# Half-empty 64-row passes of the third weight, run in pairs in the two row halves of the array

## The chip, the cores and the metric

The kernel runs on one core of a Trainium2 chip. The metric is the device time of one execution, in microseconds (us). Three runs of the kernel before took 371.08, 371.08 and 371.23 us; their median is 371.08.

The engines go by the profile's names: PE is the matrix engine (PEld its weight loads, which are instructions of their own), DVE the vector engine, ACT the scalar engine, POOL the general one, SP the engine that issues most DMAs. SBUF is the memory of 128 partitions in which tiles lie; PSUM is the smaller one that PE writes to, with 8 banks of 128 x 512 fp32.

## The reference

An input of 2048 tokens by D = 448 channels goes through two branches that are mixed by a gate. Branch `a` is a long convolution (a state-space filter). Branch `b` is what the change touches:

```python
h = _gelu(_layernorm(x) @ w1)                 # D x D
hs = shifted(h) @ w2                          # four channel groups moved by +1, -1, +2, -2 tokens
x1 = x + hs
h2 = _gelu(_layernorm(x1) @ w3) @ w4          # D x F, then F x D, F = 1792
b = x1 + h2
out = g * a + (1 - g) * b                     # g = sigmoid(sum(x * gate_w))
```

D = 448 is three tiles of 128 rows and one of 64. That last tile of 64 rows is the change's subject.

## The kernel before

**Precision.** Every matmul of a weight is made of three products in the type fp32r. An operand is split into a high part (rounded to fp32r) and a low part (what is left): `w3h`, `w3l` for the weight, `XH`, `XL` for the input. high x high, low weight x high input, and high weight x low input are added in one PSUM bank.

**The 64 rows.** The contraction over 448 channels takes four tiles, k = 0 to 3. In tile k = 3 only 64 rows are real. The kernel fills the other half: the weights are stored twice (rows 0 to 63 and again 64 to 127), and `XH[:, 3]` holds the input's high part in rows 0 to 63 and its low part in rows 64 to 127. So one pass of `w3h[:, 3]` over `XH[:, 3]` gives high x high and high x low together, which is why `XL` has three tiles only. The pass of `w3l[:, 3]` over the same tile gives low x high in its first half, and low x low in its second, a product that is left out for all other tiles.

**Units.** The work is cut into 72 units (line 455): 16 of kind `a` (w1 and w2, four channel groups in each of four blocks of 512 tokens), then 56 of kind `d` (w3 and w4: 14 tiles of F in each of four blocks). For a unit of kind `d`, `first(n)` makes 11 passes of 512 columns into a bank `p1` (L478), ACT applies the gelu into `uf` (L539) and copies it into `uh` (L549), DVE forms the low part `ul` (`act_tail`, L569), and `second(n)` makes 12 passes of 448 columns into the four banks `acc0` to `acc3` (L603), which stay open over the 14 units of a block. At a block's end `residual` adds them to the tokens `xs` on DVE.

**Order.** All is written out by hand, in program order for each engine. A loop over n (line 1217) issues, in this order: DVE's low part of the next unit (`act_tail(n + 1)`, for n from 14 on; before that it comes after the `after` list), tasks of the lists `before` and `after`, `first(n + 2)`, gelu and copy of unit n + 2, the list `between`, some steps of the filter's recurrence (`ssm_some`, DVE scans with ACT scalings), the list `late`, and `second(n)`. Each engine works through its own instructions in that order; semaphores between them follow from the tiles. The lists hold the splitting of w3 and w4 (`part_hi` on ACT, `part_lo` on DVE), the layernorm of x1 for the next block (`norm_...`), and the filter's preparation. ACT splits into the high part, DVE subtracts to get the low one.

**Buffers that matter here.** Three PSUM banks go round under the tag `p1`, one is called `misc`, four are `acc`. In SBUF `uh` and `ul` have three buffers each.

The first unit of kind `d` is number 16; `first(16)` is issued in the loop's step 14, behind `second(13)` and ahead of `second(14)`. Its layernormed input comes back from a turn through DRAM into `NT_`, and `norm_hi` (L448, ACT) and `norm_lo` (L409, L410, DVE) fill `XH` and `XL`.

Of the kernel before, what the change touches and what calls it, by code (L numbers as in the profile page):

```python
# [8 lines left out]
F32 = mybir.dt.float32  # L9
F32R = mybir.dt.float32r  # L10
I32 = mybir.dt.int32
AF = mybir.ActivationFunctionType
# [8 lines left out]
TB = 512  # L21
NB = L // TB
# [6 lines left out]
NF = F // 128  # L29
# [6 lines left out]
LAG = 2  # L36
# [143 lines left out]
def mixer_and_small_steps(ctx, tc, xs, gg, okm, x, xT, xb, x0, w1, w2, w3, w4, gate, par, logdt, dskip, ident, out):  # L180
    nc = tc.nc

    big = ctx.enter_context(tc.tile_pool(name="big", bufs=1))
    wk = ctx.enter_context(tc.tile_pool(name="wk", bufs=2))
    ps = ctx.enter_context(tc.tile_pool(name="ps", bufs=2, space=PSUM))
# [13 lines left out]
    w3l = big.tile([128, 4, F], F32R, name="w3l")  # L199
# [173 lines left out]
    XH, XL = {}, {}  # L373
# [71 lines left out]
    def norm_hi(b, i):  # L445
        if i == 0:
            hl_tiles(("d", b))
        nc.scalar.activation(XH["d", b][:, :, i * 128:(i + 1) * 128], NT_[b, i], AF.Copy)  # L448

    def weigh(b, i):  # L450
        j = NT * b + i
        nc.scalar.activation(xs[:, j, :], xs[:, j, :], AF.Copy, scale=gs[:, j:j + 1])


    units = [("a", b, g) for b in range(NB) for g in (0, 2, 1, 3)] + \
            [("d", b, f) for b in range(NB) for f in range(NF)]
    w4 = dict(src=w4)
    W4 = {}
    P1, UF, UH, UL, ACC = {}, {}, {}, {}, {}

    def first(n, bank="p1", seq=None, stop=True):

        kind, b, i = units[n]
        xh, xl = XH[kind, b], XL[kind, b]
        if kind == "a":
            wh, wl = (w1d, None) if i == 2 else (w1h[:, TI[i]], w1l[:, TI[i]])
            o = HALO - SHIFT[i]
        else:
            wh, wl = (w[:, :, i * 128:(i + 1) * 128] for w in (w3h, w3l))
            o = 0  # L470
        fresh = n not in P1
        if fresh:
            P1[n] = ps.tile([128, TB], F32, name="p1", tag=bank, bufs=3 if bank == "p1" else 1)
        p = P1[n]
        every = [(w, x_, k, 0, TB) for x_, ks in ((0, (0, 1, 2)), (0, (3,)), (1, (0, 1, 2))) for w in range(2 - x_)
                 for k in ks if not w or wl is not None]
        for q, (w, x_, k, t0, t1) in enumerate(seq or every):
            nc.tensor.matmul(p[:, t0:t1], (wl if w else wh)[:, k, :], (xl if x_ else xh)[:, k, o + t0:o + t1],  # L478
                             start=(q == 0 and fresh), stop=stop if q + 1 == len(seq or every) else False)
# [15 lines left out]
    def mul_ops(n):  # L495

        kind, b, i = units[n]
        p, o = P1[n], b * TB + HALO - SHIFT[i]
        MUL.add(n)
        if i == 2:  # L500
            if n not in UF:
                act_add(n, False)
                yield
                act_add(n, True)
                yield
            nc.vector.tensor_mul(UF[n][:GD], UF[n][:GD], rb[:GD, o:o + TB])
        else:
            UF[n] = wk.tile([128, TB], F32, name="uf")
            nc.vector.tensor_mul(UF[n], p, rb[:, o:o + TB])
        yield  # L510
# [4 lines left out]
    def head_ops(n):  # L515
        kind, b, i = units[n]
        if kind == "a" and n not in MUL:
            yield from mul_ops(n)
        UH[n] = wk.tile([128, TB], F32R, name="uh", bufs=3)
        if kind == "a" and i == 2:  # L520
            nc.scalar.activation(UF[n][:GD], UF[n][:GD], AF.Gelu_apprx_tanh)
            yield
        elif kind == "a":
            UL[n] = wk.tile([128, TB], F32R, name="ul", bufs=3)
            o, sk = SHIFT[2] - SHIFT[i], skew[:, TI[i], :]
            uf, UF[n] = UF[n], big.tile([128, TB], F32, name="ug", tag="w4bl")
            nc.scalar.activation(UF[n], uf, AF.Gelu_apprx_tanh)
            yield
            if n:
                nc.scalar.activation(UF[n][:GX, :o], sk[:, SKEW - o:], AF.Gelu_apprx_tanh)  # L530
                yield
            nc.scalar.activation(UF[n][:GX, o:], uf[:GX, :TB - o], AF.Gelu_apprx_tanh)
            if b + 1 < NB:
                EDGE[n] = sk, uf[:GX, TB - SKEW:]
            yield
        else:
            UL[n] = wk.tile([128, TB], F32R, name="ul", bufs=3)
            UF[n] = wk.tile([128, TB], F32, name="uf")
            nc.scalar.activation(UF[n], P1[n], AF.Gelu_apprx_tanh)  # L539
            yield  # L540
# [14 lines left out]
    def act_head(n, later=False):  # L555
        drain(head_ops(n))
        if not later:
            drain(copy_ops(n))

    def act_copy(n):  # L560
        drain(copy_ops(n))

    def act_tail(n):
        kind, b, i = units[n]
        uf = UF.pop(n)
        if kind == "a" and i == 2:
            nc.vector.tensor_sub(UH[n][GD:], uf[:GD], f32(UH[n])[:GD])
        else:
            nc.vector.tensor_sub(UL[n], uf, f32(UH[n]))  # L569
# [161 lines left out]
        nc.vector.tensor_reduce(rk[:, 4:5], rk[:, 0:4], axis=AX.X, op=OP.min)  # L731

    def ssm_mask():
        p = ps.tile([128, 1], F32, name="misc", bufs=1)
        nc.tensor.matmul(p, one.to_broadcast([128, 128]), rk[:, 4:5], start=True, stop=True)
        nc.vector.tensor_copy(rk[:, 5:6], p)
        nc.vector.tensor_scalar(okm, rk[:, 5:6].to_broadcast([128, 16]), 127.5, None, op0=OP.is_ge)
        nc.vector.copy_predicated(nu.rearrange("p a b -> p (a b)"), okm, nuf.rearrange("p a b -> p (a b)"))
# [83 lines left out]
    def at(n, fn, *a, when=after):  # L822
        when.setdefault(n, []).append((fn, a))

    def run(when, n):
        for fn, a in when.pop(n, []):
            fn(*a)
# [184 lines left out]
    def first_head_ops():  # L1012

        UH[0] = wk.tile([128, TB], F32R, name="uh", bufs=3)
        UL[0] = wk.tile([128, TB], F32R, name="ul", bufs=3)
        uf, ug = UF[0], big.tile([128, TB], F32, name="ug", tag="w4bl")
        UG.append(ug)
        o = SHIFT[2] - SHIFT[0]
        for a_, c in HALVES:
            nc.scalar.activation(ug[:, a_:c], uf[:, a_:c], AF.Gelu_apprx_tanh)  # L1020
            yield
            q = max(a_, o)
            nc.scalar.activation(ug[:GX, q:c], uf[:GX, q - o:c - o], AF.Gelu_apprx_tanh)  # L1023
            yield
            nc.scalar.activation(UH[0][:, a_:c], ug[:, a_:c], AF.Copy)
            yield
        P1.pop(0)
        nc.scalar.activation(skew[:, TI[0], :], uf[:GX, TB - SKEW:], AF.Copy)
        yield
# [155 lines left out]
    for b in range(NB):  # L1185
        s0 = (7, 18, 31, 46)[b]
        for i in range(NT):
            n = s0 + (3, 4, 5, 3)[b] * (i // 2)
            if b:
                at(n, norm_d, b, i, when=late if b == 3 else after)  # L1190
                at(n + 1, norm_turn, b, i)
                at(n + 2, norm_fetch, b, i)
            q, when = n + (4 if b in (1, 2) else 3), late if b == 3 else before
            if b:
                at(q, norm_hi, b, i, when=when)
                at(q, norm_lo, b, i, when=when)
            at(max(s0 + i + 8, 28 + i // 2), weigh, b, i)
    at(16, ssm_par, 0)
    at(25, ssm_par, 1, when=late)
    at(17, ssm_exp, 0)  # L1200
# [14 lines left out]
    with tc.manual_schedule():  # L1215
        begin()
        for n in range(4, len(units)):
            if n >= 4 * NB - 2 and n + 1 < len(units):
                act_tail(n + 1)
            run(before, n)  # L1220
            spent = sum(cost.get(fn, 0.0) for when in (after, late) for fn, _ in when.get(n, []))
            run(after, n)
            if n < 4 * NB - 2 and n not in (7, 11):
                act_tail(n + 1)
            if n + LAG < len(units):
                first(n + LAG)
                if units[n + LAG][::2] == ("a", 2):
                    act_add(n + LAG, False)
            if n in (7, 11):
                second(n)  # L1230
                act_tail(n + 1)
            if n + LAG in UF:
                act_add(n + LAG, True)
            if n < OWN:
                run(between, n)
            if n + LAG < len(units) and n not in (6, 10):
                act_head(n + LAG, True)
            run(between, n)
            if n + LAG < len(units) and n not in (6, 10):
                act_copy(n + LAG)  # L1240
            if n >= OWN:
                ssm_some(n, 3.75 - (2.2 if units[n][2] == NF - 1 else 0.0) - spent)
            run(late, n)
            if n < len(units) - 2 and n not in (7, 11):
                second(n)
        last_two()
# [55 lines left out]
```

## Time and profile before

| | |
|---|---|
| timed runs | 371.08, 371.08, 371.23 us |
| span of the profiled execution, from the first to the last instruction | 368.9 us |
| median of the timed runs less that span: what lies around it | 2.2 us |
| DMA queues, all together | 46.14 MB, 125 GB/s mean |
| ACT's idle time ahead of the gelu of L539, ended by PE | 113.2 us in 49 waits |
| DVE's idle time ahead of the `ul` of L569, ended by ACT's `uh` | 23.0 us in 17 waits |
| smallest and largest time of a pass of 448 columns over `ul` and `w4h` | 357 and 373 ns |

The profile gives the span of one execution and no total of its own; a sum is therefore made on the span, and the 2.2 us are added to compare it with timed runs. Times in a row of the timeline are the start from the span's beginning and how long the record lasts; "x3" merges three instructions in a row, and the time is then of all of them. The record of a matmul is longer than the distance to the next, since matmuls are pipelined. A bracket at a row's end names the idle time of that engine just before, and what ended it. Groups show busy time in all, the mean of one in ns, and idle time before them.

### The profile page before, as it was taken

What the parts mean: (1) busy time and instruction counts of PE and PEld (TensorE: products, weight loads), DVE (VectorE), ACT (ScalarE), POOL (GpSimd) and SP (SyncE); (2) the same over time, 40 slices, a digit from 0 to 9 for tenths busy, and PEclk for the clock granted to TensorE, in tenths of its full rate; (3) what the DMA queues carried; (4) which work ended last, traced back from release to release, by engine and by line L of the source; (5) the groups of instructions that cost most, each with busy time, mean ns of one, the idle gap of its engine ahead of it and who ended that gap; (6) DMA issues with size and microseconds to landing.
All of it is one profiled execution on the core that took longest, in us unless ns stands there. A gap on an engine that the chain in (4) does not pass through costs nothing.

```text
span 368.9 us, 5308 instructions
## 1 busy us (share of the span) xinstructions
PE 363.4 (99%) x1734; PEld 314.3 (85%) x1734; DVE 308.1 (84%) x571; ACT 215.9 (59%) x383; POOL 63.3 (17%) x176
## 2 busy tenths in 40 slices
PE   8999999999999999999999999999999999999995
PEld 4988888888888888888888888888888888888885
DVE  4999979797999997378799899998789999998533
ACT  5987668777684637944274774554756645455220
POOL 1000432000300000110013433224243234000000
PEclk9999999999999999999999999999999999999999
DMA  7994116626948064001833514457385611361213
GB/s 258 393 398 157 38 65 124 134 88 251 390 134 203 0 116 156 0 0 52 178 107 77 89 28 94 114 165 131 83 131 121 179 16 28 79 179 30 64 50 105
DMA packets 88479, 46.14 MB, mean 125 GB/s; under 512 B 67200, under 2 KB 82944, under 8 KB 87808
## 3 DMA queue, kind: packets, MB, share of 16 engines
q1 hardware_dynamic: 88016, 45.27, 45.6%
q10 hardware_dynamic: 432, 0.49, 0.4%
q8 instruction: 15, 0.25, 0.3%
q14 instruction: 16, 0.13, 0.1%
HBM read 34.74 MB, written 11.01 MB: 124 GB/s over the span
## 4 chain that ended last, share of the span: by engine, by line
PE 93%; DMA 4%; ACT 1%; DVE 0%; ACTq 0%; SPq 0%; issue 0%
PE p L478 46%; PE acc L603 45%; DMA raw<-xb_in 2%; DMA xs<-x_in 2%; PE acc L638 1%; ACT xh L394 1%; PE p L638 0%; PE misc L363 0%; DVE xh L401 0%; ACT uf L996 0%; ACTq L268 0%; DVE uf L1007 0%; SPq L279 0%; ACT ug L1020 0%; ACT ug L1023 0%
## 5 line engine op out<-in xcount | busy, mean ns | idle before, releaser
L539 ACT ACTIVATE uf<-p 128x512 f32<-128x512 f32 x56 | 33.4, 597 | 113.3 <-PE p L478 113.2
L478 PE MATMUL p<-xh,w3l 128*128 128x512 f32 x224 | 70.1, 394 | 0.0
L478 PE MATMUL p<-xh,w3h 128*128 128x512 f32 x224 | 70.1, 394 | 0.0
L758 DVE TENSOR_TENSOR_SCAN z<-z,carry 128x512 f32<-128x512 f32 x48 | 61.5, 1282 | 4.2 <-POOL z L752 0.5
L603 PE MATMUL acc<-w4l,uh 128*128 128x448 f32 x216 | 56.3, 367 | 0.0
L603 PE MATMUL acc<-w4h,uh 128*128 128x448 f32 x216 | 56.0, 365 | 0.0
L603 PE MATMUL acc<-w4h,ul 128*128 128x448 f32 x216 | 55.8, 364 | 0.0
L569 DVE TENSOR_TENSOR ul<-uf,uh 128x512 fp32r<-128x512 f32 x56 | 38.1, 681 | 20.1 <-ACT uh L549 20.0
L478 PEld LDWEIGHTS p<-xh,w3l 128*128 128x128 f32 x224 | 42.1, 188 | 9.8
L478 PE MATMUL p<-xl,w3h 128*128 128x512 f32 x168 | 47.7, 392 | 0.0
L478 PEld LDWEIGHTS p<-xh,w3h 128*128 128x128 f32 x224 | 42.1, 188 | 6.6
L603 PEld LDWEIGHTS acc<-w4h,uh 128*128 128x128 f32 x216 | 40.5, 188 | 6.0
L603 PEld LDWEIGHTS acc<-w4h,ul 128*128 128x128 f32 x216 | 40.6, 188 | 3.5
L603 PEld LDWEIGHTS acc<-w4l,uh 128*128 128x128 f32 x216 | 40.6, 188 | 3.4
L753 ACT ACTIVATE z<-zs,nu 128x512 f32<-128x512 f32 x64 | 42.3, 710 | 0.6 <-DMA zs<-xT_in 0.6
L478 PEld LDWEIGHTS p<-xl,w3h 128*128 128x128 f32 x168 | 31.5, 188 | 7.2
L549 ACT ACTIVATE uh<-uf 128x512 fp32r<-128x512 f32 x56 | 35.4, 633 | 1.8
L752 POOL COPY z<-carry 128x1 f32<-128x1 f32 x48 | 32.1, 679 | 16.0 <-DVE zs L764 15.9
L760 POOL COPY carry<-z 128x1 f32<-128x1 f32 x48 | 13.1, 273 | 105.7 <-DVE z L758 105.0
L344 POOL TENSOR_TENSOR t<-r 128x4 f32<-128x4 f32 (+1 forms) x5 | 3.1, 627 | 117.4 <-DVE r L343 117.4
L603 PE MATMUL acc<-w2l,uh 128*128 128x448 f32 x64 | 19.9, 368 | 0.0
L758 DVE TENSOR_TENSOR_SCAN z<-z,carry,zero 128x512 f32<-128x512 f32 x16 | 19.9, 1247 | 0.0
(207 smaller groups left out, 541.8 us busy)
## 6 DMA issues: line engine op xcount, KB each, us to landing
zs<-xT_in SPq DMA_DIRECT2D x4, 1024.0 KB, 8.3
yd<-yt SPq DMA_DIRECT2D x56, 64.0 KB, 2.0
ysb<-yd SPq DMA_DIRECT2D x16, 224.0 KB, 2.7
raw<-xb_in SPq DMA_DIRECT2D x3, 1032.0 KB, 12.6
raw<-w_in SPq DMA_DIRECT2D x3, 1024.0 KB, 5.6
xd<-xt SPq DMA_DIRECT2D x16, 192.0 KB, 2.1
xr<-xd SPq DMA_DIRECT2D x16, 192.0 KB, 3.1
raw<-w_in SPq DMA_DIRECT2D x3, 896.0 KB, 4.6
```

The source lines that it names most:

```text
L344: eng.tensor_mul(t, y, y)
L394: nc.scalar.activation(XH["a", b][:, k, :], raw[b][:, k, :], AF.Copy)
L478: nc.tensor.matmul(p[:, t0:t1], (wl if w else wh)[:, k, :], (xl if x_ else xh)[:, k, o + t0:o + t1], start=(q == 0 and fresh), stop=stop i ...
L539: nc.scalar.activation(UF[n], P1[n], AF.Gelu_apprx_tanh)
L549: nc.scalar.activation(UH[n], UF[n], AF.Copy)
L569: nc.vector.tensor_sub(UL[n], uf, f32(UH[n]))
L603: nc.tensor.matmul(ACC[j], (UL if p == 2 else UH)[n][:, t], wl if p == 1 else wh, start=first_, stop=last_)
L638: nc.tensor.matmul(acc, (UL if p == 2 else UH)[m][:, t], (wl if p == 1 else wh)[:, c], start=q == last and m == n and p == 0, stop=m > n a ...
L752: nc.gpsimd.tensor_copy(z4[:, m, 0:1], carry[:, k, m:m + 1])
L753: nc.scalar.activation(z4[:, m, 1:], ZS[b][:, k, :], AF.Copy, scale=nu[:, k, m:m + 1])
L758: nc.vector.tensor_tensor_scan(z, z, up, carry[:, k, m:m + 1], OP.add, OP.add)
L760: nc.gpsimd.tensor_copy(carry[:, k, m:m + 1], z[:, TB - 1:])
```

## The change

The pass of `w3l[:, 3]` is no longer made in `first` for units of kind `d`. Instead, a new function `tails` makes it for up to four units at once (14 units of a block: 4, 4, 4 and 2), before `first` of the first of them. It uses only the 64 rows that carry low weight x high input; low x low of that tile is no longer computed. Even units of a group use rows 0 to 63 of `w3l` and of `XH`. Odd ones use rows 64 to 127 of `w3l` (the second copy of the weights) and a new tile `xt3`, in whose rows 64 to 127 `spread_tail` puts a copy of the high part (ACT, once per block). Each pass of `tails` opens the bank of its unit, and `first` then adds to it; three banks of a group are `p1`, the fourth is `misc`. For this `ssm_mask` moves from `misc` to `p1`, and `ul` gives up one of three buffers for the room of `xt3`.

```diff
+    def spread_tail(b):
+        XT[b] = big.tile([128, TB], F32R, name="xt3", tag="xt3")
+        nc.scalar.activation(XT[b][64:], XH["d", b][:64, 3, :TB], AF.Copy)
...
+    def tails(n):
+
+        kind, b, i = units[n]
+        for m in range(4 if i + 4 <= NF else 2):
+            last = m == 3
+            p = P1[n + m] = ps.tile([128, TB], F32, name="p1", tag="misc" if last else "p1", bufs=1 if last else 3)
+            t = slice((i + m) * 128, (i + m + 1) * 128)
+            if m % 2:
+                nc.tensor.matmul(p, w3l[64:, 3, t], XT[b][64:], start=True, stop=False)
+            else:
+                nc.tensor.matmul(p, w3l[:64, 3, t], XH[kind, b][:64, 3, :TB], start=True, stop=False)
...
-                 for k in ks if not w or wl is not None]
+                 for k in ks if not w or wl is not None and not (k == 3 and kind == "d")]
...
-            UL[n] = wk.tile([128, TB], F32R, name="ul", bufs=3)
+            UL[n] = wk.tile([128, TB], F32R, name="ul", bufs=2)
...
-        p = ps.tile([128, 1], F32, name="misc", bufs=1)
+        p = ps.tile([128, 1], F32, name="p1", tag="p1", bufs=3)
...
+    for b in range(NB):
+        at((13, 27, 41, 55)[b], spread_tail, b)
...
+                if units[n + LAG][0] == "d" and units[n + LAG][2] % 4 == 0:
+                    tails(n + LAG)
                 first(n + LAG)
```

Lines behind the insertions move by 6 to 22: `first` is L496 instead of L478, `second` L621 instead of L603, the gelu L557, the copy L567, the low part L587, the splits L958 and L961. `tails` is L475 (odd units) and L477 (even units), `spread_tail` L454.

On PE, in step 14, the end of `second(13)` and `first(16)` stood like this before (`p_1043` is unit 16's bank, `acc` are the banks of `second`; a bracket names the engines or DMAs that a row waits for):

```order
L603 MATMUL acc_995<-w2l,uh 128x448
L603 MATMUL acc_999<-w2l,uh 128x448
L478 MATMUL p_1043<-xh,w3h 128x512 [waits PE_49]
L478 MATMUL p_1043<-xh,w3h 128x512
L478 MATMUL p_1043<-xh,w3h 128x512 [waits Activation_49]
L478 MATMUL p_1043<-xh,w3l 128x512 x2
L478 MATMUL p_1043<-xh,w3l 128x512 [waits DVE_49]
L478 MATMUL p_1043<-xh,w3h 128x512
L478 MATMUL p_1043<-xh,w3l 128x512
L478 MATMUL p_1043<-xl,w3h 128x512 x3
```

and stand like this in the change (`p_1045`, `p_1047`, `p_1049` and `p_1051` are the banks of units 16 to 19, `xt_1009` is the copy):

```order
L621 MATMUL acc_995<-w2l,uh 128x448
L621 MATMUL acc_999<-w2l,uh 128x448
L477 MATMUL p_1045<-xh,w3l 128x512 [waits DVE_49,PE_49]
L475 MATMUL p_1047<-xt_1009,w3l 128x512 [waits Activation_49]
L477 MATMUL p_1049<-xh,w3l 128x512 [waits DVE_49]
L475 MATMUL p_1051<-xt_1009,w3l 128x512
L496 MATMUL p_1045<-xh,w3h 128x512 x3
L496 MATMUL p_1045<-xh,w3l 128x512 x3
L496 MATMUL p_1045<-xh,w3h 128x512
L496 MATMUL p_1045<-xl,w3h 128x512 x3
```

Four passes stand ahead of `first(16)` now, the second of them with a wait for ACT and the third with one for DVE; `first` has ten passes instead of eleven.

On ACT the copy that this second pass reads stands behind the splits of step 13, and ahead of the gelu of unit 15 (`ug`, with its short pieces for shifted channels), in the change:

```order
L567 ACTIVATE uh<-ug 128x512 [waits PE_49,Activation_49]
L958 ACTIVATE w4h_701<-raw 128x896
L958 ACTIVATE w3h<-raw 128x2x512 [waits DMAHW6_49]
L454 ACTIVATE xt_1009<-xh 64x512
L545 ACTIVATE ug<-uf 128x512 [waits DVE_49,Activation_49]
L548 ACTIVATE ug<-skew 16x4 [waits Activation_49]
L550 ACTIVATE ug<-uf 16x508
```

The row at L454 is new there; the others keep their order.

On DVE, around the low part of unit 16 (the second `ul` row here), the rows before are these:

```order
L569 TENSOR_TENSOR ul<-ug,uh 128x512 [waits Activation_49]
L943 TENSOR_TENSOR w4l_702<-raw,w4h_701 128x896
L943 TENSOR_TENSOR w3l<-raw,w3h 128x2x512 [waits DMAHW6_49]
L569 TENSOR_TENSOR ul<-uf,uh 128x512 [waits Activation_49]
L943 TENSOR_TENSOR w3l<-raw,w3h 128x2x512
```

and those of the change:

```order
L587 TENSOR_TENSOR ul<-ug,uh 128x512 [waits Activation_49]
L961 TENSOR_TENSOR w4l_702<-raw,w4h_701 128x896
L961 TENSOR_TENSOR w3l<-raw,w3h 128x2x512 [waits DMAHW6_49]
L587 TENSOR_TENSOR ul<-uf,uh 128x512 [waits DVE_49,PE_49,Activation_49]
L961 TENSOR_TENSOR w3l<-raw,w3h 128x2x512
```

The order is the same; unit 16's low part now also waits for PE, since its buffer is that of unit 14, which `second(14)` reads.

More of the change, by code (lines that the diff above doesn't have):

```diff
@@ L448, in norm_hi @@
         nc.scalar.activation(XH["d", b][:, :, i * 128:(i + 1) * 128], NT_[b, i], AF.Copy)
+    XT = {}
+    def spread_tail(b):
+        XT[b] = big.tile([128, TB], F32R, name="xt3", tag="xt3")
+        nc.scalar.activation(XT[b][64:], XH["d", b][:64, 3, :TB], AF.Copy)
     def weigh(b, i):
@@ L536, in head_ops @@
         else:
-            UL[n] = wk.tile([128, TB], F32R, name="ul", bufs=3)
+            UL[n] = wk.tile([128, TB], F32R, name="ul", bufs=2)
             UF[n] = wk.tile([128, TB], F32, name="uf")
@@ L1014, in first_head_ops @@
         UH[0] = wk.tile([128, TB], F32R, name="uh", bufs=3)
-        UL[0] = wk.tile([128, TB], F32R, name="ul", bufs=3)
+        UL[0] = wk.tile([128, TB], F32R, name="ul", bufs=2)
         uf, ug = UF[0], big.tile([128, TB], F32, name="ug", tag="w4bl")
```

## Prediction

> **What bounds the kernel now.** I read the page's busy shares first, then its chain of waits, then stretches of the timeline.
>
> ```profile
> PE 363.4 (99%) x1734; PEld 314.3 (85%) x1734; DVE 308.1 (84%) x571; ACT 215.9 (59%) x383; POOL 63.3 (17%) x176
> PEclk9999999999999999999999999999999999999999
> PE 93%; DMA 4%; ACT 1%; DVE 0%; ACTq 0%; SPq 0%; issue 0%
> 80.55:85.54 4.99, 4.99 (x25) 4.32 (x24) 2.55 (x4) 4.89 (x9) 0.00 (x0) 1.00 0.66 211
> 225.30:295.13 69.83, 69.83 (x324) 60.53 (x322) 62.62 (x77) 40.31 (x67) 21.68 (x45) 1.00 0.61 134
> ```
>
> TensorE is busy in 99% of the span at full clock, and the chain that ended last runs over it for 93%. The last two rows are stretches of the window view (length, then busy time of PE, PEld, DVE, ACT and POOL): one unit, and fourteen units of the steady part. PE is busy in all of both. So a unit costs 69.83 / 14 = 4.99 us, nothing hides a PE delay, and every PE saving counts until another engine is late; DVE is next, at 62.62 / 14 = 4.47 us a unit.
>
> What fills a unit is seen at the place where the second kind of unit begins (timeline of PE: start, time, instruction, count).
>
> ```profile
> 80.14 0.57 PE L603 MATMUL acc<-w2l,uh 128*128 128x448 f32 x2
> 80.55 0.85 PE L478 MATMUL p<-xh,w3h 128*128 128x512 f32 x3
> ...
> 81.94 0.40 PE L478 MATMUL p<-xh,w3h 128*128 128x512 f32 x1
> 82.17 0.39 PE L478 MATMUL p<-xh,w3l 128*128 128x512 f32 x1
> 82.41 0.86 PE L478 MATMUL p<-xl,w3h 128*128 128x512 f32 x3
> 83.10 0.36 PE L603 MATMUL acc<-w2h,uh 128*128 128x448 f32 x1
> ```
>
> From 80.55 to 83.10 stand eleven passes of 512 columns: 2.55 / 11 = 0.232 us each, though the record of one is 0.39 long, so matmuls overlap. The two of 448 columns before them are 0.57 - 0.36 = 0.21 apart; I use 0.20, since twelve fill 4.99 - 2.55. The pass at 82.17 is the one that the change takes out.
>
> **The change part by part.** *What it removes.* In each of the 56 units of the second kind that pass goes: 56 x 0.232 = 13.0 us. *What it adds on PE* is 28 pairs of 64-row passes, in 12 groups of four and 4 of two. If two halves really run together, a pair costs one pass, and 28 x 0.232 = 6.5 us is the most that can be won.
>
> *The switch of the array's shape.* Every group makes PE go from 128-row passes to 64-row ones and back. The trace holds one such change of tile, by columns: four products for the first tokens at L845, 2 columns wide, recorded as eight passes. PE first, then the weight loads.
>
> ```profile
> 11.96 0.28 PE L478 MATMUL p<-xh,w1h 128*128 128x256 f32 x1
> 12.17 0.39 PE L845 MATMUL pe<-w1r,xz 128*2 128x32 f32 x8
> 12.49 0.39 PE L478 MATMUL p<-xl,w1h 128*128 128x256 f32 x1
> ...
> 12.17 0.26 PEld L845 LDWEIGHTS pe<-w1r,xz 128*2 128x2 f32 x8
> 12.49 0.30 PEld L478 LDWEIGHTS p<-xl,w1h 128*128 128x128 f32 x2
> ...
> 31.87 0.60 PE L363 MATMUL misc<-idt,r 128*128 128x128 f32 x4
> ...
> 200.22 0.62 PEld L478 LDWEIGHTS p<-xh,w3h 128*128 128x128 f32 x3
> 200.41 0.86 PE L478 MATMUL p<-xh,w3h 128*128 128x512 f32 x3
> ```
>
> Elsewhere weights load beside the matmul before theirs: of the last two rows the load starts 0.19 before its pass. At the change of shape they don't: the first load comes at 12.17, 0.21 after the last full matmul started and 0.07 before its record ends (11.96 + 0.28); and the way back is alike, 12.49 against 12.17 + 0.39 = 12.56. The shape of the array changes only when the matmuls in it are nearly out, and the next weights load in the open. A load of 128 columns takes 0.11: four small matmuls stand 0.11 apart ((0.60 - 0.27) / 3). So, by the records of 0.36 and 0.39, the first 64-row pass starts 0.36 - 0.07 + 0.11 = 0.40 after the last 448-column pass, not 0.20; and the next full pass 0.39 - 0.07 + 0.11 = 0.43 after the last 64-row pass, not 0.23. **Each switch costs 0.20**. No row shows a switch of row halves: from below its price is 0, from above I keep 0.20, and I take the upper end as the nearest row. Inside a group the second half can start only when its own weights are in, 0.11 later, and that stagger stays to the end of the group (bounds 0 and 0.23, the latter meaning that halves don't overlap at all).
>
> A group of four thus costs 2 x 0.20 + 0.11 and saves 2 x 0.23: +0.05. A group of two saves 0.23: +0.28. Eleven of the first kind (the twelfth is next) and four of the second: 0.5 + 1.1 = **+1.6 us**. The Trainium skill, TensorEngine Tiling (Array Packing), Tiling Modes (Key Properties), says that changing the tiling mode, unlike changing the tile, drains the TensorE; the L845 rows agree, for columns. The same skill's TensorE: Matmul & The Clock Gate, Part 3, gives starts about 4 ns apart for tiles in different row groups; by that figure the stagger would vanish and the sum be some 1.6 us less. No run so far shows it.
>
> *The first group waits.* Its second pass reads the copy that `spread_tail` makes on ACT, and on ACT that copy stands behind two weight splits.
>
> ```profile
> 81.36 0.95 ACT L940 ACTIVATE w4h<-raw 128x896 fp32r<-128x896 f32 x1
> 82.20 1.05 ACT L940 ACTIVATE w3h<-raw 128x1024 fp32r<-128x1024 f32 x1
> 83.15 0.62 ACT L527 ACTIVATE ug<-uf 128x512 f32<-128x512 f32 x1
> ...
> L546 ACT ACTIVATE uh<-uf 64x512 fp32r<-64x512 f32 x4 | 2.5, 628 | 0.1
> ...
> 82.10 0.68 DVE L509 TENSOR_TENSOR uf<-p,rb 128x512 f32<-128x512 f32 x1
> ...
> 208.77 0.64 ACT L549 ACTIVATE uh<-uf 128x512 fp32r<-128x512 f32 x1
> 209.44 0.70 DVE L569 TENSOR_TENSOR ul<-uf,uh 128x512 fp32r<-128x512 f32 x1 [0.16 <-ACT uh L549]
> ```
>
> The copy takes the place of the gelu at 83.15 and, as a 64x512 copy, 0.63: it ends at 83.78, and a waiter sees that 0.03 later (208.77 + 0.64 to 209.44). PE gets there at about 80.8 and stands: everything behind is queued on PE, and all later stages wait for it. At 83.81 the second weights load, 83.92 the second pass, 84.03 the third, 84.15 the fourth (the second must leave its half), and 0.43 later, at 84.58, the full passes begin that began at 80.55. Of these 4.03, four passes of 0.23 were due anyway: **+3.1 us**. The third pass takes the bank of unit 15, read by DVE till 82.10 + 0.68 = 82.78; the wait for ACT covers that.
>
> *The second group* takes the one-buffer bank of unit 19, whose gelu is late.
>
> ```profile
> 98.34 1.28 ACT L688 ACT_TABLE_LOAD   x1 [2.03 <-DMA pk<-par_in]
> ...
> 101.58 0.60 ACT L539 ACTIVATE uf<-p 128x512 f32<-128x512 f32 x1
> ...
> 88.57 1.22 DVE L943 TENSOR_TENSOR w3l<-raw,w3h 128x1024 fp32r<-128x1024 f32 x1
> 89.86 0.34 SPq L685 DMA_DIRECT2D pk<-par_in  x1
> ```
>
> This gelu ends at 102.18, and hangs on a DMA that SP issues once the split at 88.57 is done. With `ul` in two buffers the tail (`act_tail`) ahead of that split waits for PE's `second` of unit 14, which ends near 89.5 now; the split starts at 90.2 instead of 88.57, and the gelu ends near 103.8. PE reaches its fourth pass at about 104.0, 3.1 late: no stall, by 0.2. From the third group on the cover is wide: the gelu ends 1.6 before the next unit begins.
>
> ```profile
> 203.16 0.60 ACT L539 ACTIVATE uf<-p 128x512 f32<-128x512 f32 x1 [2.48 <-PE p L478]
> ...
> 205.40 0.86 PE L478 MATMUL p<-xh,w3h 128*128 128x512 f32 x3
> ...
> 267.86 0.66 DVE L569 TENSOR_TENSOR ul<-uf,uh 128x512 fp32r<-128x512 f32 x1
> ...
> 274.36 0.98 PE L603 MATMUL acc<-w4h,ul 128*128 128x448 f32 x4
> ...
> 149.39 0.60 ACT L539 ACTIVATE uf<-p 128x512 f32<-128x512 f32 x1
> ```
>
> *What costs nothing.* With two `ul` buffers each tail waits for the `second` two units before it, and scans, residuals and splits queue behind it on DVE. In the latest case of the trace (267.86 to 268.52, read at 274.36) 5.8 us of cover are left, the wait can move DVE back by about one, and 4.47 of work fit in a unit. The other three spreads stand in ACT's idle time; the one ahead of unit 29's gelu (149.39) moves it by 0.6 into the group at 150.35: 0.1. `ssm_mask` in another bank changes no wait, since that bank's reader is two units old.
>
> **Sum:** 3.1 + 0.5 + 1.1 + 0.1 = +4.8 us on the span of 368.9, giving 373.7. What lies around the span is 371.1 - 368.9 = 2.2 against the median of the runs, so **375.9**.
>
> **The rivals.** With c for a switch and s for the stagger the whole is 31 c + 15 s - 3.0 (31 switches count, since the entry of the first group lies in its wait).
>
> 1. *Row halves are free to switch*: c = s = 0, since row groups leave the columns' paths as they are, and weights load beside the passes before. Then -3.0, **368.1**, faster; with s = 0.11 it decides at c = 0.04. Against it stand the L845 rows; for it, that these show columns only.
> 2. *The shape drains but weights load during the drain*: c = 0.20 - 0.11 = 0.09: 2.8 + 1.6 - 3.0 = +1.4, **372.5**.
> 3. *Both halves load their weights at once* and start together: c = 0.20, s = 0: 6.2 - 3.0 = +3.2, **374.3**. Against it: in all rows one load follows the other.
> 4. *The halves don't run together* (the change doesn't do what it says): no pair saves anything, 15 groups cost 0.40 each, and the first 3.3, with the 0.1: +9.4, **380.5**. For it: matmuls on PE start in order, and no row shows two at once.
> 5. *The copy comes in time*: then the third pass still waits for DVE till 82.8, and the first group costs 2.0 instead of 3.1: **374.8**. Against it speaks ACT's order.
>
> **How the numbers follow.** Chances: forecast 0.43, free switch 0.17, loads in the drain 0.13, start together 0.08, no overlap 0.13, copy in time 0.06. Only the first rival lies outside the range of 371.9 to 380.7, which covers the bounds of c and s otherwise. What a measurement here can tell from no change is 0.2%, 0.74 us. Faster by more: 0.14 of the free switch's 0.17. Within: the other 0.03, and 0.03 of rival 2. Slower: the remaining 0.80.
>
> **What would show it.** The wait: PE idle from about 81 to 83.8, ended by ACT's copy at L454. The switch: the first 64-row load 0.29 after the last full pass, and the first full load 0.32 after the last 64-row pass. The overlap: starts at L475 and L477 0.11 apart in pairs, not 0.23. The steady unit: four units with a group in about 20.0 us, as before. I am wrong if four units take 19.5 or less (rival 1), or if the first group doesn't wait.

## The result and the profile after

The change is slower. The medians are 377.36 us (four runs, 377.15 to 378.46) against 371.12 us (four runs of the kernel before, 371.08 to 371.23): a ratio of 1.0172 with a 95% interval of 1.0158 to 1.0187, or **+6.24 us**. The forecast was 375.9 in a range of 371.9 to 380.7. The profiled execution has a span of 375.5 us against 368.9. Two executions of all those reported here, one of the kernel before (516.35 us) and one of the last kernel below (734.42 us), lie far outside; they count in the medians, but in no range and no ratio.

The page of the changed kernel, busy shares, granted clock by slices, and the chain that ended last:

```profile
PE 366.8 (98%) x1734; PEld 308.1 (82%) x1734; DVE 308.9 (82%) x571; ACT 219.1 (58%) x387; POOL 65.2 (17%) x176
PEclk9999999998999999999999999999999999999999
PE 80%; DVE 6%; ACT 6%; DMA 5%; issue 1%; SPq 1%; ACTq 0%; DVEq 0%
```

PE is still busy in 98% of the span, but the chain now leaves it for DVE, ACT and DMAs, 17% of the span together where it was 5%. And one slice of the clock row, the tenth, has an 8. The waits view (time in all, how often, the longest) names the first of the new waits:

```profile
DVE ul L587 <- PE acc L621: 15.9, 12, 4.1
...
PEld p L496 <- issue: 5.2, 16, 0.4
PEld p L477 <- issue: 5.0, 16, 0.4
...
PE p L475 <- ACT xt L454: 2.8, 1, 2.8
```

One wait for the copy; 16 exits from groups (L496) and 16 entries (L477) at which the weight loads stand still for 0.3 to 0.4 each and the view names nothing that they wait for ("issue"); and a wait of DVE's low part for PE, where before that instruction waited only for ACT's `uh`: this is what the third `ul` buffer had covered.

**Where the 6.24 us are.** The window view cuts the span at the first passes of groups: first the changed kernel, then the one before between the same passes (length, then busy time of PE, PEld, DVE, ACT, POOL, the granted clock, DMA share, GB/s).

```profile
76.73:105.89 29.16, 26.29 (x112) 21.37 (x110) 21.03 (x34) 19.62 (x29) 1.97 (x2) 0.94 0.57 199
155.78:176.47 20.69, 20.23 (x93) 16.83 (x92) 12.37 (x29) 13.31 (x24) 2.82 (x15) 1.00 0.00 0
246.65:266.53 19.88, 19.88 (x95) 16.75 (x94) 16.82 (x21) 11.02 (x19) 6.49 (x13) 1.00 0.65 142
286.40:296.53 10.13, 10.13 (x47) 8.37 (x46) 9.93 (x13) 6.67 (x12) 4.23 (x7) 1.00 0.48 130
336.46:356.43 19.97, 19.97 (x95) 16.77 (x94) 14.24 (x15) 7.53 (x13) 0.00 (x0) 1.00 0.27 60
```

```profile
76.37:100.48 24.11, 24.11 (x112) 20.86 (x111) 21.25 (x38) 16.88 (x25) 2.73 (x6) 1.00 0.66 237
150.35:170.27 19.92, 19.92 (x93) 17.28 (x92) 13.29 (x31) 11.97 (x22) 2.81 (x15) 1.00 0.00 0
240.28:260.22 19.94, 19.94 (x93) 17.29 (x92) 16.30 (x21) 10.90 (x18) 6.10 (x13) 1.00 0.68 146
280.17:290.14 9.97, 9.97 (x47) 8.64 (x46) 9.77 (x13) 6.03 (x11) 3.61 (x7) 1.00 0.48 133
329.99:349.91 19.92, 19.92 (x94) 17.27 (x92) 14.37 (x16) 7.65 (x13) 0.00 (x0) 1.00 0.24 56
```

| place | forecast, us | measured, us |
|---|---|---|
| first group and its four units | +3.1 | 29.16 - 24.11 = **+5.05** |
| group of unit 30, with the wait for unit 29's gelu | +0.05 + 0.1 | 20.69 - 19.92 = **+0.77** |
| the ten other groups of four | +0.5 | **-0.18**: -0.06 to -0.07 in each of the five of blocks 0 and 2; in blocks 1 and 3 once -0.01 (the stretch with the mask's matmul) and four times +0.04 or +0.05 |
| four groups of two | +1.1 | **+0.60**: 0.16, 0.20, 0.16, and about 0.08 for the last, which ends with the kernel |
| sum | +4.8 | **+6.24** |

The span grew by 6.6, not by 6.24: this execution was 0.36 late already at unit 15's first pass (76.73 against 76.37), ahead of everything that the change touches.

**The first group** on PE in the timeline (start, length, instruction; a bracket is the idle time ahead, with what ended it):

```profile
81.19 0.46 PE L477 MATMUL p<-xh,w3l 64*128 64x512 f32 x1
84.47 0.49 PE L475 MATMUL p<-xt,w3l 64*128 64x512 f32 x1 [2.82 <-ACT xt L454]
...
85.13 0.50 PE L496 MATMUL p<-xh,w3h 128*128 128x512 f32 x1
```

ACT in the same place, and two windows behind it with the granted clock of PE:

```profile
83.79 0.63 ACT L454 ACTIVATE xt<-xh 64x512 fp32r<-64x512 f32 x1
```

```profile
85.70:89.10 3.40, 3.40 (x10) 2.64 (x9) 2.57 (x3) 1.71 (x3) 0.00 (x0) 0.51 0.02 9
89.10:95.00 5.90, 5.90 (x29) 5.22 (x28) 2.43 (x4) 2.15 (x4) 0.00 (x0) 1.00 1.00 329
```

The second pass waits for the copy, as forecast; the full passes begin at 85.13. What was not forecast comes after the wait. For the 3.4 us from 85.70 on the granted clock is 0.51, though PE is busy throughout: this is the 8 in the clock row. The ten passes of unit 16 take from 85.13 to 89.06, 3.93 us; where the clock is full (the run with dummy passes, below) they take 2.41.

**A group without a wait**, passes and then loads:

```profile
225.87 0.96 PE L621 MATMUL acc<-w4h,ul 128*128 128x448 f32 x4
226.77 0.50 PE L477 MATMUL p<-xh,w3l 64*128 64x512 f32 x1
226.77 0.50 PE L475 MATMUL p<-xt,w3l 64*128 64x512 f32 x1
227.11 0.39 PE L477 MATMUL p<-xh,w3l 64*128 64x512 f32 x1
227.11 0.39 PE L475 MATMUL p<-xt,w3l 64*128 64x512 f32 x1
227.44 0.73 PE L496 MATMUL p<-xh,w3h 128*128 128x512 f32 x2
```

```profile
226.77 0.18 PEld L477 LDWEIGHTS p<-xh,w3l 64*128 64x128 f32 x1 [0.29 <-issue]
226.77 0.18 PEld L475 LDWEIGHTS p<-xt,w3l 64*128 64x128 f32 x1
226.88 0.19 PEld L477 LDWEIGHTS p<-xh,w3l 64*128 64x128 f32 x1
...
227.43 0.53 PEld L496 LDWEIGHTS p<-xh,w3h 128*128 128x128 f32 x3 [0.37 <-issue]
```

The two halves of a pair load and start at the same printed time, where a stagger of 0.11 was forecast. Inside the group loads run beside passes (226.88 under a pass that runs until 227.27); at both ends they don't: the first comes 0.29 after the last full pass started (at 226.48: 225.87 + 0.96, less the 0.36 of a record), the first of the full shape at 227.43, with none since 226.88. The passes start with these loads, and the next ones follow 0.34 and 0.33 later (227.11, 227.44) where full passes in a row follow 0.23 apart: a load that had no pass to run beside delays what comes behind it.

### The profile page after: what moved, and what is told of

Read it like the earlier page. It is cut to its first block, busy times and chain, and to the rows that moved or that the text cites. A ratio compares the mean times of both kernels' runs of the same rounds, so it can differ in the third digit from the quotient of the medians.

```text
span 375.5 us, 5321 instructions
## 1 busy us (share of the span) xinstructions
PE 366.8 (98%) x1734; PEld 308.1 (82%) x1734; DVE 308.9 (82%) x571; ACT 219.1 (58%) x387; POOL 65.2 (17%) x176
## 4 chain that ended last, share of the span: by engine, by line
PE 80%; DVE 6%; ACT 6%; DMA 5%; issue 1%; SPq 1%; ACTq 0%; DVEq 0%
PE acc L621 39%; PE p L496 37%; DMA w1r<-w_in 2%; PE p L477 2%; DMA pk<-par_in 2%; PE acc L656 1%; PE p L475 1%; DMA xr<-xd 1%; DVE gx L688 1%; ACT xh L394 1%; DVE uf L527 1%; DVE xl L409 1%; SPq L442 1%; PE p L656 0%; DVE xl L399 0%
## 5 line engine op out<-in xcount | busy, mean ns | idle before, releaser
L557 ACT ACTIVATE uf<-p 128x512 f32<-128x512 f32 x56 | 33.5, 599 | 114.2 <-PE p L496 114.2
L496 PE MATMUL p<-xh,w3h 128*128 128x512 f32 x224 | 72.2, 403 | 0.0
L587 DVE TENSOR_TENSOR ul<-uf,uh 128x512 fp32r<-128x512 f32 x56 | 38.2, 683 | 29.8 <-PE acc L621 15.9
L621 PE MATMUL acc<-w4h,ul 128*128 128x448 f32 x216 | 56.3, 366 | 0.0
L621 PE MATMUL acc<-w4l,uh 128*128 128x448 f32 x216 | 56.3, 366 | 0.0
L621 PE MATMUL acc<-w4h,uh 128*128 128x448 f32 x216 | 56.1, 365 | 0.0
L496 PEld LDWEIGHTS p<-xh,w3h 128*128 128x128 f32 x224 | 41.0, 189 | 11.7 <-issue 5.2
L496 PE MATMUL p<-xl,w3h 128*128 128x512 f32 x168 | 48.7, 399 | 0.0
L496 PE MATMUL p<-xh,w3l 128*128 128x512 f32 x168 | 48.4, 397 | 0.0
L621 PEld LDWEIGHTS acc<-w4h,uh 128*128 128x128 f32 x216 | 40.5, 188 | 6.1
L621 PEld LDWEIGHTS acc<-w4l,uh 128*128 128x128 f32 x216 | 40.6, 188 | 3.9
L621 PEld LDWEIGHTS acc<-w4h,ul 128*128 128x128 f32 x216 | 40.6, 188 | 3.2
L496 PEld LDWEIGHTS p<-xh,w3l 128*128 128x128 f32 x168 | 32.0, 190 | 7.4
L496 PEld LDWEIGHTS p<-xl,w3h 128*128 128x128 f32 x168 | 32.0, 190 | 7.4
L770 POOL COPY z<-carry 128x1 f32<-128x1 f32 x48 | 33.5, 710 | 17.0 <-DVE zs L782 16.9
L567 ACT ACTIVATE uh<-uf 128x512 fp32r<-128x512 f32 x56 | 35.4, 632 | 1.8
L621 PE MATMUL acc<-w2l,uh 128*128 128x448 f32 x64 | 20.0, 367 | 0.0
```

Source lines behind the costliest of these rows:

```text
L567: nc.scalar.activation(UH[n], UF[n], AF.Copy)
L621: nc.tensor.matmul(ACC[j], (UL if p == 2 else UH)[n][:, t], wl if p == 1 else wh, start=first_, stop=last_)
L770: nc.gpsimd.tensor_copy(z4[:, m, 0:1], carry[:, k, m:m + 1])
```

## The experiments

Each edit stands against the changed kernel unless it says otherwise. The kernel before was run again beside each batch, with medians of 371.33, 371.20 and 371.19; a ratio is against those of its own batch, with its 95% interval. Ratios are means over the timed rounds without the profiled execution, so with three rounds they can differ from the quotient of the medians by some 0.2%.

### The copy two steps earlier

```diff
-        at((13, 27, 41, 55)[b], spread_tail, b)
+        at((11, 27, 41, 55)[b], spread_tail, b)
```

> The first block's copy is issued two steps earlier on ACT, right behind the last norm_hi. My theory (the first group waits for ACT's copy, and an idle of some 3 us also halves the clock): the next late thing is DVE's product of unit 15, near 82.8 us; PE idles about 1.4 us instead of 3.3, the clock stays full, and the time is about 374.1. Rival (the slow passes behind the first group come from the change of shape, not from the idle time): they stay, 375.7. Rival (the wait is not for the copy): 377.4, as the change.

375.92 us (374.41 to 379.09), ratio 1.0149 (1.0104 to 1.0195): 1.4 less than the change by the medians, above the 374.1 that was expected, and by the ratio not to be told from the change. PE in its first group, and a window of its clock:

```profile
81.10 0.47 PE L477 MATMUL p<-xh,w3l 64*128 64x512 f32 x1
81.10 0.49 PE L475 MATMUL p<-xt,w3l 64*128 64x512 f32 x1
83.28 0.49 PE L477 MATMUL p<-xh,w3l 64*128 64x512 f32 x1 [1.69 <-DVE uf L527]
```

```profile
83.90:87.31 3.41, 3.41 (x9) 2.67 (x10) 1.66 (x3) 2.61 (x5) 0.00 (x0) 0.50 0.54 210
```

The wait for ACT is gone and the one behind it, for DVE and the bank of unit 15, shows, as expected. But the clock fell to half again, for 3.41 us, after an idle time of only 1.69. Moving the copy does not repair the group. Since the slow passes stayed, the time is also that of the rival which puts them down to the change of shape (375.7); the next run decides between the two.

### Dummy passes in the wait

```diff
+            for _ in range(13 if n + m == 16 else 0):
+                nc.tensor.matmul(p, warm[:, 0:128], warm, start=True, stop=True)
             if m % 2:
```

Thirteen passes over a bf16 tile of ones go to unit 16's bank ahead of its first pass, which opens the bank anew.

> As the change, but 13 useless bf16 passes of 512 columns stand ahead of the first group, in unit 16's bank, which the group's first pass then overwrites: PE works while it would wait. My theory (idle time halved the clock): the granted clock stays at 1.0 behind the group, its ten passes take 2.4 us instead of 3.9, and the time is about 375.9. Rival (the half clock belongs to the switch of shape, or the passes are slow for another reason): 377.4 or more.

375.96 us (375.75 to 377.39), 1.0145 (1.0122 to 1.0167), as expected. The window over what follows the wait:

```profile
85.00:89.00 4.00, 4.00 (x20) 3.48 (x19) 2.83 (x3) 3.16 (x5) 0.00 (x0) 1.00 0.18 39
```

The full passes start at 84.65 and the wait is as it was; PE is merely busy in it. The clock stays at 1.00, the ten passes take 2.41, and the time falls by 1.4 us by the medians, by 1.0 by the ratios. So the half clock is a cost of its own, set off by PE standing idle, and it is the 1.5 us of the first group that the forecast lacked.

### Without the first group

Units 16 to 19 keep their eleven passes; the first group is that of unit 20.

```diff
-                 for k in ks if not w or wl is not None and not (k == 3 and kind == "d")]
+                 for k in ks if not w or wl is not None and not (k == 3 and kind == "d" and n > 19)]
...
-                if units[n + LAG][0] == "d" and units[n + LAG][2] % 4 == 0:
+                if units[n + LAG][0] == "d" and units[n + LAG][2] % 4 == 0 and n + LAG > 19:
```

> Units 16 to 19 make their low-weight pass in the old way, with 128 rows; all other groups stay as in the change. My theory: the first group's wait and the half clock go (5.1 us), and the second group waits 1.4 us for the late gelu of unit 19, which the first wait had hidden: about 373.7. Rival (most of the loss is spread over all switches): at most 0.4 of the 6.2 us go, about 377.

373.32 us (373.09 to 375.8), 1.0083 (1.0053 to 1.0114); 373.7 was expected. Most of the +2.0 that is left is a new wait, at the second group:

```profile
102.35 0.49 PE L477 MATMUL p<-xh,w3l 64*128 64x512 f32 x1 [1.30 <-ACT uf L557]
```

Its first two passes start at 100.56, so the third comes 1.79 behind them, where it comes 0.34 behind in a group without a wait: it is 1.45 late, for the gelu of unit 19, which the first group's delay had hidden until now. The prediction had cleared this place by 0.2 for the change, and there it held. With an idle time of 1.30 the clock stayed at 1.00.

### Everything in one row half

The odd units' passes use rows 0 to 63 too, so no pair can overlap, and no copy is needed.

```diff
-                nc.tensor.matmul(p, w3l[64:, 3, t], XT[b][64:], start=True, stop=False)
+                nc.tensor.matmul(p, w3l[:64, 3, t], XH[kind, b][:64, 3, :TB], start=True, stop=False)
...
-        at((13, 27, 41, 55)[b], spread_tail, b)
+        pass
```

> All gathered passes use rows 0 to 63, with no copy into the other half: the shape changes as often as in the change, but two passes can't run side by side. My theory (in the change the halves overlap fully, and a pair costs one pass of 0.23): each group of four costs 0.46 more than in the change, each group of two 0.23, and the first waits for DVE alone: about 379.8. Rival (the gain in the change comes from fewer rows, not from overlap): the time stays near that of full rows gathered in the same way.

379.61 us (379.52 to 380.04), 1.0228 (1.0211 to 1.0245), as expected. A group without a wait:

```profile
225.82 0.50 PE L477 MATMUL p<-xh,w3l 64*128 64x512 f32 x1
...
226.94 0.96 PE L496 MATMUL p<-xh,w3h 128*128 128x512 f32 x3
```

It takes 226.94 - 225.82 = 1.12 us, the change's 227.44 - 226.77 = 0.67. The difference of 0.45 is two passes: the overlap of the halves is real and is worth all that was hoped of it. The entry and the exit are the same in both.

### Gathered, but over all 128 rows

Same groups, same order, same two `ul` buffers, but passes of the full shape, as before the change; no copy.

```diff
-                nc.tensor.matmul(p, w3l[64:, 3, t], XT[b][64:], start=True, stop=False)
+                nc.tensor.matmul(p, w3l[:, 3, t], XH[kind, b][:, 3, :TB], start=True, stop=False)
             else:
-                nc.tensor.matmul(p, w3l[:64, 3, t], XH[kind, b][:64, 3, :TB], start=True, stop=False)
+                nc.tensor.matmul(p, w3l[:, 3, t], XH[kind, b][:, 3, :TB], start=True, stop=False)
...
-        at((13, 27, 41, 55)[b], spread_tail, b)
+        pass
```

> The passes are gathered as in the change, but with 128 rows: no switch of shape, no copy, no overlap; two ul buffers stay. What is left of the change is its waits. My theory: 1.8 us for DVE's product of unit 15 in the first group and 0.7 for the gelu of unit 29: about 373.6. Rival (the waits come from the 64-row shape): 371.1.

373.66 us (373.44 to 374.85), 1.0077 (1.0057 to 1.0096), as expected. Its groups have no gap at either end (a pass every 0.23), so what it costs, +2.5, is the price of gathering alone. Most of it is the first group's wait for DVE (its four units take 21.50 instead of 19.93) and the wait for the gelu of unit 29 (20.64 instead of 19.92). The rest shows no wait at all. These are four units with a group in block 2 and in block 3:

```profile
242.87:262.82 19.95, 19.95 (x94) 17.28 (x92) 16.91 (x21) 10.90 (x18) 6.56 (x13) 1.00 0.67 145
312.79:332.85 20.06, 20.06 (x94) 17.30 (x93) 18.61 (x21) 10.45 (x18) 0.84 (x6) 1.00 0.40 98
```

In block 2 they take what they took before (19.95 against 19.94), in block 3 0.14 more (20.06 against 19.92), with PE busy throughout. So gathering costs something in block 3 that has nothing to do with the shape of the passes.

The same with three `ul` buffers (`bufs=3`, no `xt3`):

> As the run with full rows gathered, with three ul buffers and no room kept for the copy. My theory (two ul buffers make DVE wait for PE, which delays the second load of the filter's parameters, and with it the gelu of unit 29): the wait of 0.7 us at the group of unit 30 goes, about 372.9. Rival (that wait has nothing to do with ul): 373.6.

374.01 us (373.37 to 374.86), 1.0076 (1.0055 to 1.0097): no gain in the time, where about 0.7 was expected. The trace does show the effect. The group of unit 30 with two buffers, then with three:

```profile
152.16 0.40 PE L475 MATMUL p<-xh,w3l 128*128 128x512 f32 x1
152.88 0.49 PE L477 MATMUL p<-xh,w3l 128*128 128x512 f32 x1 [0.32 <-ACT uf L557]
```

```profile
152.79 0.39 PE L475 MATMUL p<-xh,w3l 128*128 128x512 f32 x1
153.02 0.39 PE L477 MATMUL p<-xh,w3l 128*128 128x512 f32 x1
```

The wait goes with the third buffer, and the four units take 20.04 instead of 20.64. Runs of one kernel spread by up to 1.5 us here, and a cost of 0.6 is beyond what these few timings resolve.

**Two `ul` buffers in the kernel before** (`bufs=2`, nothing else):

> The kernel before with two ul buffers and nothing else changed. My theory: DVE waits for PE in many units, the second load of the filter's parameters is issued about 0.9 us later against PE, but no group takes unit 29's bank early: 371.1. Rival (two ul buffers cost time by themselves): 371.8 or more, with PE waiting for DVE or ACT.

371.58 us (370.84 to 372.35), 1.0011 (0.9999 to 1.0023). Alone, the missing buffer costs nothing that can be told. In the trace it does delay the second load of the filter's parameters, issued at 138.9 and so 11.2 ahead of unit 30 (150.12), where the kernel before has 11.9 (138.41 and 150.35); but no pass on PE waits for it.

### The groups moved

To dodge both bad places, groups of four from the third, seventh and eleventh unit of each block on; the first two units of a block go the old way.

```diff
-        for m in range(4 if i + 4 <= NF else 2):
+        for m in range(4):
...
-                 for k in ks if not w or wl is not None and not (k == 3 and kind == "d")]
+                 for k in ks if not w or wl is not None and not (k == 3 and kind == "d" and i > 1)]
...
-                if units[n + LAG][0] == "d" and units[n + LAG][2] % 4 == 0:
+                if units[n + LAG][0] == "d" and units[n + LAG][2] % 4 == 2:
```

> The first two units of each block make the pass in the old way; the twelve others form three groups of four, which begin at the third, seventh and eleventh unit of a block. No group of two is left, and no group meets the late product of unit 15 or the late gelus of units 19 and 29. My theory (a group of four wins 0.05 us once nothing waits): 371.1 - 12 x 0.05 = 370.5. Rival (each switch costs 0.20 and the halves start 0.11 apart, as forecast): 371.7. Rival (two ul buffers cost time of their own): above 371.5 with PE waiting for DVE.

376.31 us (374.99 to 377.53), 1.0138 (1.0113 to 1.0164): a miss by almost 6 us. Its waits and clock:

```profile
133.87 0.49 PE L477 MATMUL p<-xh,w3l 64*128 64x512 f32 x1 [2.67 <-DVE w3l L961]
```

```profile
134.79:138.21 3.42, 3.42 (x10) 2.66 (x9) 1.28 (x5) 0.00 (x0) 0.00 (x0) 0.50 0.85 135
```

Block 0 is where `w3` is still being split, step by step, just ahead of its use. Gathering asks for the columns of four units when the first is due, and the group of unit 26 asked for columns whose low part DVE writes later. The half clock followed once more. At 188.94 the mask's small matmul waited 0.69 for a bank that the group had taken.

### No wait left

The two splits in question two steps earlier and the mask one place later (ahead of step 35 in place of inside step 34), on top of the moved groups:

```diff
-                        (24, 24, s3, (3, 0)), (24, 24, s3, (3, 2)), (26, 26, s4, (3, 0))):
+                        (22, 22, s3, (3, 0)), (22, 22, s3, (3, 2)), (26, 26, s4, (3, 0))):
...
-    at(34, ssm_mask, when=between)
+    at(35, ssm_mask, when=before)
```

> As the run with moved groups, with its two waits taken away: the split of w3's last columns is written two steps earlier (step 22), and the small matmul of ssm_mask one step later (at the head of step 35). My theory (a group of four that meets no wait takes 19.87 us for its four units instead of 19.94): twelve groups win 0.07 each, 0.8 us, and the time is about 370.4 against 371.2 for the kernel before. Rival (two ul buffers or the copies cost as much): 371.2 or more, seen against the next run.

371.28 us (370.37 to 371.86, twelve runs), 1.0000 (0.9987 to 1.0013): not the 370.4 that was expected, but the rival's time. The kernel before with the same two moves and two `ul` buffers:

> The kernel before with the same two moves and with two ul buffers, but no group and no copy: what the moves do by themselves. My theory: nothing, 371.3; so the run before this one is about 0.8 us faster than this. Rival (the moves themselves win or lose time): 370.5 or 372, and the groups are worth nothing.

371.39 us (370.55 to 371.98), 1.0001 (0.9989 to 1.0014): as expected for itself, but the 0.8 us between the two are not there. In the waits view of the version without waits PE has one row in all, from the start of the kernel:

```profile
PE pw L921 <- PEq L1316: 0.8, 1, 0.8
```

Nothing waits in its twelve groups, the clock is full, and it is as fast as the kernel before. Two windows of its span say why it is not faster:

```profile
250.18:270.06 19.88, 19.88 (x95) 16.76 (x94) 16.11 (x21) 12.16 (x20) 7.57 (x13) 1.00 0.60 107
319.86:339.83 19.97, 19.97 (x94) 16.76 (x93) 17.73 (x21) 9.84 (x17) 0.42 (x3) 1.00 0.38 96
```

Four units with a group take 0.06 less than before in block 2 and 0.05 more in block 3 (19.88 and 19.97 against 19.94 and 19.92). Blocks 0 and 1 do much the same as 2 and 3, so over twelve groups that adds up to nothing. No version tried here beats the kernel before.

## Why the prediction was right, and where its sizes were off

The direction and the main cause were right: what can be won is eaten by the switches, and the waits are on top. Point by point:

- **The switch of shape: right.** The first load came 0.29 after the start of the last full pass, and the way back 0.32 after the last 64-row pass (227.43 - 227.11), both as worked out from the L845 rows. From block 2, two switches less two passes are 19.88 - 19.94 = -0.06, so a switch is (0.46 - 0.06) / 2 = 0.20. Rivals 1 and 2 fall with this. Against full rows gathered in the same order the two blocks nearly agree, 19.88 - 19.95 = -0.07 and 19.97 - 20.06 = -0.09, and a switch comes out at about 0.19.
- **The overlap: right.** One row half alone costs two passes more per group. Rival 4 falls.
- **The stagger: mis-sized.** It was taken as 0.11, since all rows showed one load after the other; the two halves load and start together. This is what rival 3 said. That is 15 x 0.11 = 1.6 less than forecast. Of it, 1.2 arrived: the sum of the ten groups and the four pairs came to +0.42 instead of +1.6. The rest was taken by a term that the sum did not have: the five other groups of blocks 1 and 3 cost some 0.1 each more than the five of blocks 0 and 2. The Trainium skill, TensorE: Matmul & The Clock Gate, Part 3, gives starts about 4 ns apart for tiles in different row groups; in this case's trace, pairs that wait for nothing start in the same printed hundredth or the next.
- **The first group's wait: right in kind, mis-sized.** ACT's copy did hold PE, and the full passes began 0.2 later than worked out (85.13 less the 0.36 of this execution, against 84.58). But the term counted only the idle time. PE's idle time halved its clock for 3.4 us afterwards, 3.93 instead of 2.41 for ten passes: **+1.5**, shown by the dummy passes. Of the 1.95 that the term was short, these two make 1.7; the rest was not told apart. The rival "copy in time" (374.8) would have failed on the same point, as its run did.
- **The second group: right.** No stall in the change; without the first group its third pass is 1.45 late.
- **"What costs nothing": wrong, by 0.6.** The step cleared two `ul` buffers by the cover of each tail, 5.8 us. It did not follow what stands behind a tail on DVE. These are ACT and then SP of the change ahead of unit 30's group, and both in the kernel before:

```profile
149.97 0.63 ACT L454 ACTIVATE xt<-xh 64x512 fp32r<-64x512 f32 x1
151.11 1.28 ACT L706 ACT_TABLE_LOAD   x1 [0.51 <-DMA pk<-par_in]
...
154.80 1.28 ACT L557 ACT_TABLE_LOAD   x1
156.09 0.60 ACT L557 ACTIVATE uf<-p 128x512 f32<-128x512 f32 x1
```

```profile
144.57 0.35 SPq L703 DMA_DIRECT2D pk<-par_in  x1
```

```profile
144.40 1.28 ACT L688 ACT_TABLE_LOAD   x1
...
138.41 0.35 SPq L685 DMA_DIRECT2D pk<-par_in  x1
```

That group begins at 155.78 (150.35 before, the second rows of the windows above). So the DMA was issued 11.94 ahead of unit 30 before, and 11.21 ahead in the change. The chain runs from a tail that waits for PE, over the gate's sums behind it on DVE, to this DMA, which SP issues when they are done, and whose data ACT awaits with a table load; the gelu of unit 29 comes after a second table load. It ends at 156.69, and the group, which needs that bank for its third pass, starts that pass at 156.74 instead of 156.11 (0.33 behind the first, as in the group of 226.77 to within 0.01). The term had only the spread's place on ACT (0.1); since ACT stood idle for 0.51 behind the spread until the DMA landed, the spread alone was not what held it. That the buffers do was shown on the full-row pair of kernels, where the third buffer removes the wait, and the DMA is issued 0.7 later against unit 30 with two buffers alone.

The two errors on the first group and on unit 30 (+2.0 and +0.6) and the one on the stagger (-1.2) have opposite signs. That the total is only 1.4 off, while one term alone is off by 2.0, is in part luck.

**Left open.** A group of four gains about 0.07 in blocks 0 and 2 and costs up to 0.05 in blocks 1 and 3, with and without the waits. The runs with full rows narrow it down: there gathering alone costs 0.14 in block 3 and 0.01 in block 2, with two `ul` buffers as with three. So it is neither the shape nor the buffers, but something else that comes with the gathering; no run looked further.

## What to carry to other kernels

Two half-empty passes side by side are worth one pass, but each change of the array's shape cost 0.20 us here, most of a pass of 512 columns; two pairs in a group only broke even, and one pair lost. Gathering work into a group also moves every need of its later members to the first one's time: before doing so, list for each member when its bank, its weights and its operand come free, and follow what stands behind a delayed instruction on its engine down to the DMAs. And when PE is made to wait for long in an otherwise full stretch (1.69 us was enough here, 1.48 was not), allow for a slow clock behind the wait.

## What was not expected of the hardware

- After PE had stood idle, the granted clock was 0.50 or 0.51 for 3.4 us while PE was busy: after 2.82 us of idle time in the change, 1.69 in the run with the earlier copy, 2.67 in the moved groups. After 1.30 (without the first group) and 1.48 (full rows, three `ul` buffers) it was not. The drop came 0.6 to 1.3 us after work had resumed, and in the 3.41 us just ahead of it PE had been busy for 1.27, 1.68 and 0.92 us. The Trainium skill, TensorE: Matmul & The Clock Gate, Part 1, gives half clock after an idle window of about 3.4 us, and says that this window runs freely. The length of 3.4 agrees; but here an idle time of half that length was enough in a profiled execution. Whether it is hit seems to differ between executions: the four of the earlier copy had mean clocks of 0.992 to 0.999 with times of 379.09 to 374.41, those of the change 0.991 to 0.995.
- Passes in the two row halves that wait for nothing load and start within 0.01 us of each other (226.77 for all four rows above), though their loads stand one behind the other in the program.
- Passes gathered in blocks 1 and 3 run a little slower than the same passes in blocks 0 and 2, at full clock and with PE busy throughout (20.06 and 19.95 for four units over full rows). The cause is open.
